# A longer plain stretch around the second norm, its four turns spread one to a round, and outputs split sooner

## The chip, the cores and the metric

The kernel runs on one core of one Trainium2 chip. The metric is the device time of one execution in microseconds (us); lower is better. A core has five engines that run their own instruction streams and meet at semaphores: PE (TensorE, matmuls; its weight loads are told apart as PEld), DVE (VectorE), ACT (ScalarE), POOL (GpSimd) and SP (SyncE, which here only issues DMAs). Sixteen DMA engines serve the queues of SP and POOL.

## What is computed

A transformer block with adaptive layer norms: attention with 32 heads of 16 features over 2048 tokens, then a gated feed-forward part (FFN).

```python
def _A_ref(x, wqkv, wo):              # B, S, D = 1, 2048, 512; H = 32, Dh = 16
    qkv = ... x @ wqkv ...            # q, k, v of every head
    scores = einsum("bhqd,bhkd->bhqk", q, k) * Dh ** -0.5
    o = einsum("bhqk,bhkd->bhqd", softmax(scores), v)
    return o.transpose(...).reshape(B, S, D) @ wo

def _B_ref(x, w_gate, w_up, w_down):  # F = 1792
    return (silu(x @ w_gate) * (x @ w_up)) @ w_down

sa, ca, ga, sb, cb, gb = (silu(c) @ w_mod) in six parts
h = layernorm(x) * (1 + ca) + sa
x = x + ga * _A_ref(h, A_wqkv, A_wo)
h = layernorm(x) * (1 + cb) + sb
x = x + gb * _B_ref(h, B_w_gate, B_w_up, B_w_down)
```

## The kernel before

**Units, steps, pairs.** The queries are cut into four chunks of 512 rows, the heads into eight groups of four. One group of one chunk is a unit; there are 32 units, each with 16 key tiles of 128 keys, so 512 steps in all. A step is four pairs (`pair_of`), one for each head of the group. A pair is two matmuls on PE: a *score* (L612, operands `qop,kop`), whose exponential ACT takes from a PSUM bank into an SBUF tile `pt` or `pu` (L614), and a *maximum* (L563, operands `kop,qop`), a 128x512 product whose row maximum DVE takes (L565). The maxima run 20 steps ahead of the scores, since a unit's row maxima enter its scores as extra rows of `qop`. The counter `done` counts pairs, so `done // 4` is the step.

**Value products.** `pv_step` (L627) multiplies the exponentials with v. It works in halves, one for each 256 queries: four rows of the program, one a head, which the trace shows as eight matmuls. A step owes two halves. All of a unit's 32 halves collect in one bank, bank 70 in the order below. After the last one ACT copies that bank to an SBUF tile `o` (L631), and the next unit's first value product must wait for that copy. `close_unit` then sends the unit's output on: the sums `dn` by DMA on SP (L638), their reciprocal on DVE (L642), through DRAM and back as `rb` (L643, L648), the product with `o` on POOL (L653) and the store in DRAM `o_dr` (L654). After the eighth unit of a chunk the whole chunk's output is read back (`load_o`, L767), 128 rows of 512 for each of four k, and split on POOL into a high part (L772) and a low part (L773), tiles `act`.

**Plain and filled steps.** Steps come in two kinds, and the order on every engine is the order in which this code is written. `plain(steps, tails)` has nothing but attention. It goes in windows of three pairs (`WIN`); after window w it calls `tails[w]` if there is one and then gives out `HALVES[(w - 2) % 4]` halves of value products, HALVES being (2, 1, 1, 2). So four windows are a round: two windows with double halves follow two with single ones. A `pvs` call in a plain step stops at a unit's end and gives the rest out later, so that three pairs stand between a unit's last value product and the next unit's first. `filled(places, work)` lays matmuls of the output projection or the FFN (L829) between the pairs of some steps, at `places`, and gives out all value products of these steps at their end, in one burst, without stopping at a unit's end.

**A chunk's second half.** For each of the first three chunks the main loop runs plain steps until step `STARTS[ci]`; then two `filled_tile` calls of four steps each for the output projection (`out_pair`), after each of which DVE adds the result to the residual `x2` (L860); then a plain stretch of `NORM` steps, in which the second norm is made: sums on ACT, `norm_scale` on DVE and POOL (L785 to L798), four `normalize` on POOL (L807), and four *turns*: PE transposes one k of the normalized rows into a bank that it takes from the maxima's four (L812), ACT scales it (L814), POOL splits it (L815, L816). Then the FFN's 84 filled steps. For the third chunk 12 more plain steps (`REST`) follow the stretch, in a call of their own. Each `plain` call starts its windows at w = 0 and gives one half more in its last window. In the last two windows of a call, and in filled steps, a unit's maxima are brought into `qop` by two DVE instructions and eight DMAs (`max_turned`, L588 to L602), otherwise by three small matmuls, a copy and two DMAs (`max_rows`, L570 to L581).

Of the kernel before, what the change touches and what calls it, by code (L numbers as in the profile page):

```python
# [28 lines left out]
NK = D // P  # L29
NC = 4  # L30
CW = S // NC
NG = H // 4
# [14 lines left out]
FBANKS = (3, 6)  # L47
KEEP = 7
REST = 12
NORM = 18  # L50
STARTS = (147, 275, 403)
TWO = (0, 3, 2, 2, 2, 2, 1, 0)
DOWN = (0, 3, 3, 0, 3, 3, 0, 0)
FOUR = (0, 3, 2, 1, 2, 1, 3, 0, 3, 1, 2, 1, 2, 1, 2, 0)
# [59 lines left out]
def block_kernel(ctx, tc, x, wqkv, wo, w_gate, w_up, w_down, c, w_mod, out):  # L114
    nc = tc.nc
# [422 lines left out]
    last = NC - 1  # L538
# [6 lines left out]
    def load_k(u):  # L545
        load_parts(kop[u % 3], kd, u % NG, 0, S, nc.gpsimd if u > 2 else nc.sync)

    def load_q(u):
        ci, g = divmod(u, NG)
        qop[u] = pb.tile([P, 2, CW], F32R, name="qop", tag="qop", bufs=3)  # L550
        first, second = [(nc.gpsimd, nc.sync)[k] for k in ((0, 0), (1, 1), (1, 0))[min(u, 1) + (u > 2)]]
        load_parts(qop[u], qd, g, ci * CW, (ci + 1) * CW, second, first)
# [81 lines left out]
    def out_a(u, eng):  # L634
        pv.pop(u)
        o = o_.pop(u)
        dn = pf.tile([P, 16], F32, name="dn", tag="dn", bufs=1)
        eng.dma_start(dn, o[16:P:32, :].rearrange("h (b e) -> h b e", e=16))  # L638
        return o, dn

    def out_b(u, eng, o, dn):
        nc.vector.reciprocal(dn, dn)  # L642
        eng.dma_start(d_dr[u].rearrange("h (b e) -> (h b) e", e=16), dn)  # L643
        return o,

    def out_r(u, eng, o):
        rb = pf.tile([P, CW], F32, name="rb", tag="rb", bufs=1)
        eng.dma_start(rb, d_dr[u][:, None, :].to_broadcast([4, 32, CW]))  # L648
        return o, rb

    def out_c(u, eng, mul, o, rb):
        ci, g = divmod(u, NG)
        mul.tensor_mul(rb, o, rb)  # L653
        eng.dma_start(o_dr[ci, g], rb)  # L654

    def at(i, f):
        due.setdefault(i, []).append(f)
# [282 lines left out]
    chunks = {}  # L940
    side = []
    def begin(ci):
        x2 = pf.tile([P, 4, D], F32, name="x2", tag="x2", bufs=1)
        act = [pf.tile([P, NK, CW], F32R, name=f"act{a}", tag=f"act{a}", bufs=1) for a in range(2)]
        hT = [pf.tile([P, NK, CW], F32R, name=f"act{a}", tag=f"act{a}", bufs=1) for a in range(2)]
        chunks[ci] = ch = Chunk(ci, x2, act, hT)
        ch.load_x2(nc.sync if ci else nc.gpsimd)

    def scaled(ch):
        ch.load_gu(0)  # L950
        ch.load_gu(1)
        ch.norm_scale(nc.gpsimd)
        ch.nt = [tile_mid().bitcast(F32) for _ in range(2)]
        for t in range(4):
            ch.normalize(t)
# [17 lines left out]
    def close_unit(u, i):  # L973

        if u == NU - 1:
            res[u] = out_a(u, nc.scalar)
            return
        res[u] = out_a(u, nc.sync)
        if u + 3 < NU:
            load_k(u + 3)  # L980
            load_q(u + 3)
        i0 = i if u % NG == NG - 1 else i + 3
        at(i0 + 3, lambda: res.__setitem__(u, out_b(u, nc.sync, *res[u])))
        at(i0 + 4, lambda: res.__setitem__(u, out_r(u, nc.sync, *res[u])))
        at(i0 + 5, lambda: out_c(u, nc.gpsimd, nc.gpsimd, *res.pop(u)))
        if u % NG == NG - 1:
            if u // NG:
                at(i + 4, lambda: begin(u // NG))
                at(i + 5, lambda: chunks[u // NG].load_wo())
            at(i + 7, lambda: chunks[u // NG].load_o(nc.gpsimd))  # L990
            at(i + 9, lambda: chunks[u // NG].split_o())

    at(3, lambda: begin(0))
    at(UG - 2, lambda: chunks[0].load_wo())
# [31 lines left out]
    def pair_of():  # L1026
        nonlocal done
        i = done // 4 - 1
        most = 4 * n - 4 * (LEAD - 1)
        h = (ORDER if done < most else (0, 1, 2, 3))[done % 4]  # L1030
        work = [lambda: score(i + 1, h)]
        if done < most:
            work.insert(1 - h % 2, lambda: max_one(done + 4 * (LEAD - 1)))
        for f in work:
            f()
        done += 1
        if side:
            side.pop(0)()
# [39 lines left out]
    def pvs(most, by_halves):  # L1078

        nonlocal owed  # L1080
        if by_halves:
            most, owed = most + owed, 0
        while most and halves and 4 * halves[0][0] + 8 <= done:
            i, half = halves.pop(0)
            pv_step(i, half)
            most -= 1
            if i % 16 == 15 and half:
                close_unit(i // 16, done // 4 - 1)
                if by_halves:
                    break  # L1090
        if by_halves and most and halves and 4 * halves[0][0] + 8 <= done:
            owed = most

    def turns_behind():
        for b in list(behind):
            b[0] -= 1
            if not b[0]:
                b[1]()
                behind.remove(b)

    def end_steps():
        nonlocal ended
        while ended < done // 4:
            after(ended - 1)
            ended += 1

    def plain(steps, tails=()):

        nonlocal four, bank, beside
        beside = False  # L1110
        assert steps % WIN == 0 and done % 4 == 0
        four, bank = Turn(0, 3, 1, 2), Turn(4, 5, 6)
        for w in range(4 * steps // WIN):
            beside = w > 4 * steps // WIN - 3
            for _ in range(WIN):
                pair_of()
            if w < len(tails) and tails[w]:
                tails[w](four())
            pvs((HALVES[(w - 2) % 4] if done > 8 else 0) + (w == 4 * steps // WIN - 1), True)
            turns_behind()  # L1120
            end_steps()
# [17 lines left out]
    def filled_tile(job, ch, arg):  # L1139
        one = done // 4 % 16 != 15 and done + 16 <= 4 * n - 4 * (LEAD - 1)  # L1140
        work = job(ch, arg, outs, True, one)
        for places in (FOUR,) if one else (TWO, TWO):
            filled(places, work)
# [14 lines left out]
    for ci in range(last):  # L1158
        plain(STARTS[ci] - done // 4)
        ch = chunks[ci]  # L1160
        for t0 in (0, 2):
            filled_tile(out_pair, ch, t0)
        behind.append([6, lambda: scaled(ch)])
        tails = [None] * 10
        for k in range(NK):
            tails += [lambda tp, k=k: ch.turned(tp, k), None, None]
        plain(NORM, tails)
        if ci == last - 1:
            plain(REST)
        for _ in range(len(ch.jobs) - (KEEP if ci == last - 1 else 0)):  # L1170
            job, args = ch.jobs.pop(0)
            if ci == last - 1 and args == (7,):
                plain(18 - REST)
            if job is gate_up:
                filled_tile(job, ch, *args)
            else:
                filled(DOWN, job(ch, *args, outs, True))
# [25 lines left out]
    ch, chp = chunks[last], chunks[last - 1]  # L1203
# [54 lines left out]
```

## Time and profile before

| | us |
|---|---|
| three timed runs, median (lowest to highest) | 1818.45 (1815.83 to 1818.61) |
| the profiled execution, its own time | 1815.69 |
| its span (first to last instruction) | 1813.9 |

Shares of the span that an engine is busy: PE 99%, weight loads 65%, DVE 83%, ACT 68%, POOL 25%. The granted TensorE clock was 0.999. A busy PE is not a PE at its peak, because matmuls are pipelined and a matmul that waits for its bank counts as begun. So stages are read apart, by what ended the idle time of DVE and of the weight loads in each. Steps 0 to 146 are plain apart from weight preparation that other engines do beside them. The first chunk's output projection begins at 525.8 us, its norm stretch at 552.5 us, its FFN at 599.0 us; for the second chunk at 925.1, 952.1 and 998.7 us, for the third at 1324.6, 1351.4 and (after the 12 further plain steps) 1427.0 us.

### The profile page before, as it was taken

The numbers are of one execution on the slowest core, as the hardware profiler recorded it, in microseconds if no ns is written. First come the engines' busy times: TensorE is split into PE (matmuls) and PEld (weight loads), VectorE is DVE, ScalarE is ACT, GpSimd is POOL, SyncE is SP. The second block draws the span as 40 slices with busy tenths as digits, with TensorE's granted clock in tenths as the row PEclk, the third lists the DMA queues.
The fourth block names the chain that finished last, engine by engine and source line by source line (L and its number), as shares of the span: only waits on it lengthen the run. The fifth ranks groups of instructions, "written<-read, shape, count | busy, mean of one in ns | idle before, by whom it ended". The sixth has DMA issues, their size and how long they took to land.

```text
span 1813.9 us, 41319 instructions
## 1 busy us (share of the span) xinstructions
PE 1803.1 (99%) x17036; PEld 1173.2 (65%) x17036; DVE 1506.5 (83%) x2558; ACT 1232.2 (68%) x2356; POOL 459.1 (25%) x538
## 2 busy tenths in 40 slices
PE   9999999999999999999999999999999999999999
PEld 7876444444455677777564777777564677667887
DVE  5568999999999888888999888888989988922544
ACT  4223888888889767667788766776888867773211
POOL 3612544556223111111133111111123011031200
PEclk9999999999999999999999999999999999999999
DMA  9874876667844554464455555444624555233742
GB/s 310 288 232 142 202 199 175 174 171 199 213 80 104 126 127 120 112 149 98 111 124 122 127 121 128 110 123 102 168 61 104 104 148 123 106 122 117 291 165 101
DMA packets 80705, 267.65 MB, mean 148 GB/s; under 512 B 19884, under 2 KB 24428, under 8 KB 59836
## 3 DMA queue, kind: packets, MB, share of 16 engines
q1 hardware_dynamic: 61540, 179.71, 34.1%
q0 software_dynamic: 18288, 84.49, 19.4%
q8 instruction: 134, 2.20, 0.5%
q10 hardware_dynamic: 688, 0.80, 0.1%
q14 instruction: 55, 0.45, 0.1%
HBM read 201.85 MB, written 62.13 MB: 146 GB/s over the span
## 4 chain that ended last, share of the span: by engine, by line
PE 89%; DVE 9%; ACT 1%; DMA 0%; issue 0%; SPq 0%; DVEq 0%
PE bank L627 24%; PE bank L829 20%; PE bank L612 15%; PE bank L563 13%; DVE mx L565 9%; PE bank L848 8%; PE bank L223 5%; PE bank L466 2%; PE bank L891 1%; PE bank L812 1%; DMA wm_ab<-in_w_mod 0%; PE bank L175 0%; DVE v_flat L924 0%; PE bank L577 0%; SPq L271 0%
## 5 line engine op out<-in xcount | busy, mean ns | idle before, releaser
L565 DVE TENSOR_REDUCE mx<-bank 128x1 f32<-128x512 f32 x2048 | 1259.5, 682 | 113.9 <-PE bank L563 79.7
L563 PE MATMUL bank<-kop,qop 48*128 48x512 f32 x2048 | 733.7, 425 | 0.7
L612 PE MATMUL bank<-qop,kop 50*128 50x512 f32 x2048 | 730.8, 427 | 1.9 <-ACT pt__17687 L614 0.4
L612 PEld LDWEIGHTS bank<-qop,kop 50*128 50x128 f32 x2048 | 345.6, 184 | 196.5 <-issue 34.9
L563 PEld LDWEIGHTS bank<-kop,qop 48*128 48x128 f32 x2048 | 351.1, 184 | 111.6 <-DVE mx L565 68.9
L829 PE MATMUL bank<-act,wgu 64*128 64x512 f32 x1872 | 306.2, 392 | 0.0
L829 PEld LDWEIGHTS bank<-act,wgu 64*128 64x128 f32 x1872 | 190.5, 187 | 17.8
L653 POOL TENSOR_TENSOR rb<-o,rb 128x512 f32<-128x512 f32 x31 | 39.8, 1285 | 436.0 <-DMA rb<-d_dr 349.3
L912 POOL CAST mid<-m 128x512 fp32r<-128x512 f32 x40 | 24.2, 606 | 434.1 <-DVE m L910 434.1
L829 PE MATMUL bank<-wd,mid 64*128 64x512 f32 x912 | 131.4, 391 | 0.0
L829 PEld LDWEIGHTS bank<-wd,mid 64*128 64x128 f32 x912 | 91.5, 186 | 11.7
L908 DVE SCALAR_TENSOR_TENSOR q<-th,bank 128x512 f32<-128x512 f32 x56 | 37.9, 676 | 54.7 <-ACT th L904 54.7
L904 ACT ACTIVATE th<-bank 128x512 f32<-128x512 f32 x56 | 33.5, 598 | 58.4 <-PE bank L848 58.4
L223 PE MATMUL bank<-hT,wqs 128*128 128x512 f32 x300 | 72.4, 395 | 0.4 <-DVE wqs L363 0.4
L924 DVE TENSOR_TENSOR x<-bank,x 128x512 f32<-128x512 f32 x84 | 53.9, 685 | 16.2 <-PE bank L829 16.1
L223 PEld LDWEIGHTS bank<-hT,wqs 128*128 128x128 f32 x300 | 55.4, 188 | 13.8 <-issue 1.0
L910 DVE TENSOR_TENSOR m<-bank,q 128x512 f32<-128x512 f32 x56 | 38.7, 692 | 21.4 <-PE bank L848 19.4
L913 POOL TENSOR_TENSOR mid<-m,mid 128x512 fp32r<-128x512 f32 x40 | 51.3, 1282 | 3.4
L848 PE MATMUL bank<-wd,mid 128*128 128x512 f32 x216 | 51.5, 393 | 0.0
L829 PE MATMUL bank<-wgu,act 64*128 64x512 f32 x288 | 47.9, 393 | 0.0
L848 PEld LDWEIGHTS bank<-wd,mid 128*128 128x128 f32 x216 | 40.3, 188 | 9.1 <-POOL mid L913 0.3
L848 PE MATMUL bank<-kop,kop 128*128 128x512 f32 x192 | 45.4, 393 | 0.0
(6304 smaller groups left out, 5219.7 us busy)
## 6 DMA issues: line engine op xcount, KB each, us to landing
wgu<-gu_dr SPq DMA_DIRECT2D x48, 1024.0 KB
wd<-wd_dr SPq DMA_DIRECT2D x28, 1024.0 KB
kop<-kd SPq DMA_DIRECT2D x33, 768.0 KB
kop<-kd POOLq DMA_DIRECT2D x29, 768.0 KB, 9.3
gu_dr<-wgu POOLq DMA_DIRECT2D x14, 1024.0 KB, 13.5
kd<-prt SPq DMA_DIRECT2D x16, 512.0 KB
qd<-prt SPq DMA_DIRECT2D x16, 512.0 KB
kop<-gu_dr SPq DMA_DIRECT2D x8, 1024.0 KB
```

What stands on the lines that cost most here:

```text
L223: nc.tensor.matmul(pt, lhs(a, k), rhs(b, k), start=(n == 0), stop=(n == 3 * nk - 1))
L563: nc.tensor.matmul(pm, qop[u][rows, s, qt * P:(qt + 1) * P], kop[u % 3][rows, s, kc * CW:(kc + 1) * CW], start=True, stop=True)
L565: nc.vector.tensor_reduce(mx[u][:, b, s, qt, kc:kc + 1], pm, op=ALU.max, axis=AX.X)
L612: nc.tensor.matmul(sp, kop[u % 3][rows, h // 2, kt * P:(kt + 1) * P], qop[u][rows, h // 2, :], start=True, stop=True)
L627: nc.tensor.matmul(pv[u][32 * h:32 * h + 32, cols], v_flat[:, e0:e0 + 32], p_[h][:, cols], start=(kt == 0 and half == 0), stop=(kt == 15), ...
L653: mul.tensor_mul(rb, o, rb)
L829: mm = nc.tensor.matmul(outs[e], lhs(e, a, k)[rows], rhs(b, k)[rows], start=(ph == 0 and j == 0), stop=(j == z and (ph == 1 or trade)), sk ...
L848: nc.tensor.matmul(outs[e], lhs(e, a, k), rhs(b, k), start=(j == 0), stop=(j == z))
L908: nc.vector.scalar_tensor_tensor(q, th, 1.0, outs[0], op0=ALU.add, op1=ALU.mult)
L910: nc.vector.tensor_mul(m32, outs[1], q)
L913: (nc.gpsimd if slow else nc.vector).tensor_sub(mid[:, 1, :], m32, mid[:, 0, :].bitcast(F32))
L924: nc.vector.tensor_add(ch.x2[:, t, :], outs[e], ch.x2[:, t, :])
```

## The change

The three `STARTS` are 3 steps earlier and `NORM` is 3 steps longer, so the FFN begins at the same step as before: what was 147 plain, 8 filled, 18 plain becomes 144, 8, 21. The turns go from windows 10, 13, 16, 19 to 11, 15, 19, 23, which is the first single-half window of each of four rounds. For the third chunk the 21 and the 12 steps become one call of 33. The chunk's object is made earlier (`begin` at i + 1), three quarters of the chunk's output are read back and split at i + 1 and i + 2, and only the last quarter, which holds the last two units, waits for i + 7 and i + 9; the load of `x2` stays at i + 4.

```diff
-NORM = 18
-STARTS = (147, 275, 403)
+NORM = 21
+STARTS = (144, 272, 400)
...
         chunks[ci] = ch = Chunk(ci, x2, act, hT)
-        ch.load_x2(nc.sync if ci else nc.gpsimd)
+        if not ci:
+            ch.load_x2(nc.gpsimd)
...
             if u // NG:
-                at(i + 4, lambda: begin(u // NG))
+                at(i + 1, lambda: begin(u // NG))
+                at(i + 4, lambda: chunks[u // NG].load_x2(nc.sync))
                 at(i + 5, lambda: chunks[u // NG].load_wo())
-            at(i + 7, lambda: chunks[u // NG].load_o(nc.gpsimd))
-            at(i + 9, lambda: chunks[u // NG].split_o())
+            at(i + 1, lambda: chunks[u // NG].load_o(nc.gpsimd, range(NK - 1)))
+            at(i + 2, lambda: chunks[u // NG].split_o(range(NK - 1)))
+            at(i + 7, lambda: chunks[u // NG].load_o(nc.gpsimd, (NK - 1,)))
+            at(i + 9, lambda: chunks[u // NG].split_o((NK - 1,)))
...
-        tails = [None] * 10
+        tails = [None] * 11
         for k in range(NK):
-            tails += [lambda tp, k=k: ch.turned(tp, k), None, None]
-        plain(NORM, tails)
-        if ci == last - 1:
-            plain(REST)
+            tails += [lambda tp, k=k: ch.turned(tp, k), None, None, None]
+        plain(NORM + (REST if ci == last - 1 else 0), tails)
```

Three places show how the instructions stand now. The first is PE at the end of unit 8, whose last key tile falls at step 143 to 145. Before, this is in the plain steps ahead of the output projection:

```order
L627 MATMUL bank_70<-pu__6045,v_flat 32x256
L563 MATMUL bank_64<-kop_971,qop 128x512 [waits DVE_49]
L612 MATMUL bank_67<-qop,kop_88 128x512 [waits Activation_49]
L563 MATMUL bank_65<-kop_971,qop 128x512 [waits DVE_49]
L612 MATMUL bank_68<-qop,kop_88 128x512 [waits Activation_49]
L612 MATMUL bank_69<-qop,kop_88 128x512 [waits Activation_49]
L563 MATMUL bank_63<-kop_971,qop 128x512 [waits DVE_49]
L627 MATMUL bank_70<-pt__6052,v_flat 32x256 [waits Activation_49]
L627 MATMUL bank_70<-pt__6064,v_flat 32x256
```

Now it is in the burst behind the first four filled steps (the same unit's last half, then the next unit's first):

```order
L627 MATMUL bank_70<-pt__6020,v_flat 32x256
L627 MATMUL bank_70<-pt__6040,v_flat 32x256
L627 MATMUL bank_70<-pt__6033,v_flat 32x256
L627 MATMUL bank_70<-pu__6045,v_flat 32x256
L627 MATMUL bank_70<-pt__6056,v_flat 32x256 [waits Activation_49]
L627 MATMUL bank_70<-pt__6074,v_flat 32x256
L627 MATMUL bank_70<-pt__6061,v_flat 32x256
L627 MATMUL bank_70<-pu__6083,v_flat 32x256
```

The wait for ACT's copy stood behind three pairs and now stands directly behind the value product that the copy needs; six halves of the burst and the next filled steps are queued behind it. The same happens at units 16 and 24.

The second place is PE at the first turn of the first chunk. Before, the turn is followed by a double half (these four rows and the same four again):

```order
L563 MATMUL bank_63<-kop_1658,qop 128x512 [waits DVE_49]
L812 MATMUL bank_66<-ident,mid 128x128 [waits DVE_49,Pool_49]
L812 MATMUL bank_66<-ident,mid 128x128 [waits Pool_49] x3
L627 MATMUL bank_70<-pt__6702,v_flat 32x256
L627 MATMUL bank_70<-pt__6714,v_flat 32x256
L627 MATMUL bank_70<-pt__6707,v_flat 32x256
L627 MATMUL bank_70<-pu__6731,v_flat 32x256
```

Now one half follows, and then the next pairs:

```order
L612 MATMUL bank_67<-qop,kop_971 128x512 [waits Activation_49]
L812 MATMUL bank_63<-ident,mid 128x128 [waits DVE_49,Pool_49]
L812 MATMUL bank_63<-ident,mid 128x128 [waits Pool_49] x3
L627 MATMUL bank_70<-pt__6642,v_flat 32x256
L627 MATMUL bank_70<-pt__6662,v_flat 32x256
L627 MATMUL bank_70<-pt__6647,v_flat 32x256
L627 MATMUL bank_70<-pu__6667,v_flat 32x256
L612 MATMUL bank_68<-qop,kop_971 128x512 [waits Activation_49]
L563 MATMUL bank_66<-kop_1658,qop 128x512 [waits DVE_49]
```

Of the four turns before, two stood ahead of double halves and two ahead of single ones; now all four stand ahead of single ones.

The third place is POOL ahead of the first output projection. Before, the product for the chunk's last unit comes first and then the whole chunk is read and split:

```order
L653 TENSOR_TENSOR rb<-o,rb 128x512 [waits DMAHW4_49,DMASW5_49,Activation_49]
L654 DMA o_dr<-rb 128x512 [waits DMASW0_49,Pool_49]
L767 DMA act_1757<-o_dr 128x1x512
L767 DMA act_1757<-o_dr 128x1x512 [waits DMASW2_49]
L767 DMA act_1757<-o_dr 128x1x512 [waits DMASW3_49]
L767 DMA act_1757<-o_dr 128x1x512 [waits DMASW4_49,DMASW0_49]
L772 CAST act_1756<-act_1757 128x512 [waits DMASW1_49]
L773 TENSOR_TENSOR act_1757<-act_1757,act_1756 128x512 [waits Pool_49]
```

Now three loads stand right behind the loads of `kop` and `qop` for the unit three further on, three splits follow them, and only one quarter comes after the product (from the third split on):

```order
L772 CAST act_1756<-act_1757 128x512 [waits DMASW2_49]
L773 TENSOR_TENSOR act_1757<-act_1757,act_1756 128x512 [waits Pool_49]
L653 TENSOR_TENSOR rb<-o,rb 128x512 [waits DMAHW4_49,DMASW5_49,Activation_49]
L654 DMA o_dr<-rb 128x512 [waits DMASW3_49,Pool_49]
L767 DMA act_1757<-o_dr 128x1x512 [waits DMASW4_49,DMASW3_49]
L772 CAST act_1756<-act_1757 128x512 [waits DMASW4_49]
```

Three of the four reads of `o_dr` have moved ahead of the product on POOL's queue, and with them their splits.

## The prediction

> **What bounds the kernel now.** I read the page first: PE has work all the time, and the chain that ended last is PE's, but 9% of it is DVE's maxima. The third row is the group that PE's loads wait for.
>
> ```profile
> PE 1803.1 (99%) x17036; PEld 1173.2 (65%) x17036; DVE 1506.5 (83%) x2558; ACT 1232.2 (68%) x2356; POOL 459.1 (25%) x538
> PE 89%; DVE 9%; ACT 1%; DMA 0%; issue 0%; SPq 0%; DVEq 0%
> L565 DVE TENSOR_REDUCE mx<-bank 128x1 f32<-128x512 f32 x2048 | 1259.5, 682 | 113.9 <-PE bank L563 79.7
> ```
>
> An average over stages hides which engine is late, so I cut the time by stage: plain steps ahead of the first output projection, that projection, and the norm stretch behind it (columns: length, then busy time of PE, weight loads, DVE, ACT, POOL).
>
> ```profile
> 440.00:516.00 76.00, 76.00 (x773) 36.79 (x776) 76.00 (x131) 66.61 (x133) 33.34 (x35) 1.00 0.70 178
> 525.84:552.47 26.63, 26.63 (x294) 19.32 (x290) 22.83 (x39) 22.24 (x45) 1.49 (x2) 1.00 0.35 57
> 552.47:599.00 46.53, 45.98 (x459) 22.20 (x455) 44.60 (x78) 41.74 (x85) 16.59 (x30) 1.00 0.53 126
> ```
>
> In plain steps DVE never rests: 76.00 of 76.00. In the projection it has 3.8 us to spare, and PE sets the pace. In the norm stretch, plain steps as well, DVE loses 1.9 us. The groups by line say what a maximum costs and who ended those waits; the first row is of 440 to 516 us, the second of the norm stretch.
>
> ```profile
> L565 DVE TENSOR_REDUCE mx<-bank 128x1 f32<-128x512 f32 x127 | 76.2, 679 | 0.0
> L565 DVE TENSOR_REDUCE mx<-bank 128x1 f32<-128x512 f32 x72 | 44.3, 683 | 3.4 <-PE bank L563 3.0 <-PE bank L612 0.2
> ```
>
> A maximum takes 76.2 / 127 = 0.60 us and a plain step four of them, 2.4 us. So in plain steps a microsecond counts when DVE is given work or is left without a product; in filled steps, when PE is. DVE's timeline of the turns shows its idle times in brackets, and that of the weight loads where the four turns (L812) stand.
>
> ```profile
> 574.25 5.48 DVE L565 TENSOR_REDUCE mx<-bank 128x1 f32<-128x512 f32 x9 [0.47 <-PE bank L563]
> 580.11 7.53 DVE L565 TENSOR_REDUCE mx<-bank 128x1 f32<-128x512 f32 x12 [0.39 <-PE bank L563]
> 587.56 0.24 DVE L642 RECIPROCAL dn<-dn 128x16 f32<-128x16 f32 x1
> 587.74 3.83 DVE L565 TENSOR_REDUCE mx<-bank 128x1 f32<-128x512 f32 x6
> 591.75 1.89 DVE L565 TENSOR_REDUCE mx<-bank 128x1 f32<-128x512 f32 x3 [0.18 <-PE bank L612]
> ...
> 572.10 0.42 PEld L812 LDWEIGHTS bank<-ident,mid 128*128 128x128 f32 x4 [0.48 <-POOL mid L807]
> 577.98 0.42 PEld L812 LDWEIGHTS bank<-ident,mid 128*128 128x128 f32 x4 [0.41 <-DVE mx L565]
> 584.06 0.42 PEld L812 LDWEIGHTS bank<-ident,mid 128*128 128x128 f32 x4 [0.24 <-DVE mx L565]
> 590.02 0.42 PEld L812 LDWEIGHTS bank<-ident,mid 128*128 128x128 f32 x4 [0.37 <-DVE mx L565]
> ```
>
> The two turns ahead of double halves (572.10, 577.98) leave DVE idle for 0.47 and 0.39 us; the two ahead of single ones for nothing and for 0.18. The first also waited 0.48 us for POOL's normalized rows.
>
> **The change, term by term.** *The turns.* Before, 0.47 + 0.39 + 0.18 = 1.04 us a chunk. After, all four stand as the last two did, which cost 0.18 together, 0.09 each: 0.36 us. The first is a window later and no longer early for POOL. That gives back 0.68 us a chunk, 2.0 for three. Ends: every turn costs 0.18 (gain 0.32 a chunk, 1.0 in all), or none costs anything (3.1).
>
> *The unit's end that moves into a burst.* Units 8, 16 and 24 end some two steps behind the new start of the projection, so their last value product, before in plain steps, lies inside a burst. What PE does at such an end today, in plain steps (first row), and how long the copy takes when it follows a burst with nothing between (the other rows):
>
> ```profile
> 921.97 0.11 PEld L627 LDWEIGHTS bank<-pt__11309,v_flat 128*32 128x32 f32 x1 [0.37 <-ACT o L631]
> ...
> 611.97 0.38 PE L627 MATMUL bank<-pt__7173,v_flat 128*32 128x256 f32 x1
> 612.18 0.38 PE L627 MATMUL bank<-pt__7173,v_flat 128*32 128x256 f32 x1
> 612.65 0.59 ACT L631 COPY o<-bank 128x512 f32<-128x512 f32 x1 [2.70 <-PE bank L627]
> ```
>
> Value passes follow each other by 0.21 us (611.97, 612.18), so the next would begin at 612.39; the copy ends at 612.65 + 0.59 = 613.24. In a burst PE would stand 0.85 us, and the projection is the stage where PE sets the pace: +0.85 a chunk, +2.6 in all. Ends: nothing, if it costs as little as the 0.37 us wait in plain steps, which DVE's work covers; and 0.85 + 0.59 = 1.4 a chunk, 4.3 in all, if the copy finds ACT in another instruction of its size. I take the middle row, the only one with copy and burst side by side.
>
> *The unit's output chain, three steps later.* The reciprocal of units 8, 16 and 24 falls into plain steps instead of filled ones. From 587.56 to the next maximum at 587.74 it costs DVE 0.18 us: +0.5 for three, between 0 and 0.5.
>
> *The third chunk's joined call.* Where the 18 steps ended and 12 began, DVE's timeline has this:
>
> ```profile
> 1398.51 0.69 DVE L565 TENSOR_REDUCE mx<-bank 128x1 f32<-128x512 f32 x1 [0.37 <-PE bank L563]
> 1399.12 0.17 DVE L593 SCALAR_TENSOR_TENSOR parts<-m,parts 128x16 fp32r<-128x16 f32 x1
> 1399.32 0.21 DVE L595 STREAM_TRANSPOSE turned<-parts 128x32 f32<-128x32 f32 x1
> 1399.46 3.04 DVE L565 TENSOR_REDUCE mx<-bank 128x1 f32<-128x512 f32 x5
> ```
>
> The extra half of the last window goes (0.37 us), and away from a call's end the maxima are brought over by matmuls, so two DVE instructions go (1399.12 to 1399.46, 0.34). PE's three small matmuls come instead, in steps where it has some time; I take -0.6, between 0 and -0.7.
>
> *What costs nothing.* The 3 steps leave one plain stretch and join another: 3 x 2.4 us less and more. POOL's three early splits, 5.8 us a chunk, lie beside plain steps in which it is busy 33 of 76 us. For the fourth quarter the question is whether it comes in time; the second chunk has the least room (POOL's timeline, then that of the loads and of PE where the projection begins, then POOL's of the first chunk):
>
> ```profile
> 915.83 0.59 POOL L767 DMA_DIRECT2D act<-o_dr  x1 [5.52 <-DMA o_dr<-rb]
> 916.41 0.63 POOL L772 CAST act<-act 128x512 fp32r<-128x512 f32 x1
> DMA to landing us min/median/max: 4.1/4.1/4.1
> 925.14 0.18 PEld L612 LDWEIGHTS bank<-qop,kop 50*128 50x128 f32 x1 [0.67 <-ACT pu__11395 L614]
> 929.42 0.87 PE L829 MATMUL bank<-wgu,act 64*128 64x512 f32 x6
> ...
> 518.78 1.28 POOL L773 TENSOR_TENSOR act<-act,act 128x512 fp32r<-128x512 f32 x1
> ```
>
> The last read is issued at 915.83 and lands 4.1 us later, at 919.9. Now its split follows at once: the high part is there at 919.9 + 0.63 = 920.5. PE wants this quarter in the group of six at 929.42, which is 4.3 us behind the projection's first step at 925.14. With a start three steps (7.2 us) earlier that is 922.2. So 1.7 us of room and no wait. In the first chunk (last row) the last split ended at 520.1; without the three ahead of it that is 514.3, and the new start is at 525.8 - 7.2 = 518.6.
>
> *Sum.* -2.0 + 2.6 + 0.5 - 0.6 = +0.5 us. Against the profiled execution's own 1815.69 (span 1813.9 and 1.8 around it) that is 1816.2. The three timed runs, 1818.45, 1815.83 and 1818.61, are 1817.63 on average, so a median can come from either end; I predict 1817.63 + 0.5 = 1818.1. The terms' ends add to -3.3 (0 - 3.1 + 0.5 - 0.7) and +3.8 (4.3 - 1.0 + 0.5 + 0).
>
> **The rivals.** *Slower: a small transfer behind the early reads.* The three early reads, 768 KB, now enter POOL's queue with the loads of `kop` and `qop`, in the very microseconds in which `dn` of the chunk's last unit is fetched. Rows of that window, the second chunk's:
>
> ```profile
> DMA packets 818, 2.52 MB, mean 158 GB/s; under 512 B 353, under 2 KB 353, under 8 KB 625
> kop<-kd POOLq DMA_DIRECT2D x1, 768.0 KB, 9.6
> 882.00 0.58 POOL L487 DMA_DIRECT2D qop<-qd  x1 [0.15 <-issue]
> L638 SPq DMA_DIRECT2D dn<-o x1: 589/589/589, 882.1 to 882.1; - x1
> L642 DVEq EVENT_SEMAPHORE  x1: 21/21/21, 891.2 to 891.2; - x1
> L642 DVE RECIPROCAL dn<-dn x1: 244/244/244, 892.9 to 892.9; 128x16 f32<-128x16 f32 x1
> ```
>
> DVE's sequencer found `dn` landed at 891.2, the reciprocal began at 892.9: 1.7 us of room at least. At 158 GB/s 768 KB take 4.9 us. If `dn` waits for all of it, DVE stands 3.2 us in a plain step, 9.6 for three chunks: 1828. It decides from 1.7 us of delay on. For it: `kop` itself needed 9.6 us. Against: POOL would issue the reads from 882.6 on, SP issued `dn` at 882.1, half a microsecond ahead. The Trainium skill (DMA: Bandwidth & Descriptors, Queues, rings and completion order) says that an engine takes turns between queues, a packet from each; by it `dn` would wait for one packet of POOL's queue at most, and the sum stays 1818.1. The trace has it land 9.1 us after its issue or sooner, which does not settle it. I give one chance in eight to a delay that counts, mostly a partial one (1821 to 1824).
>
> *Faster: no burst stall.* If PE's wait in the burst is made up, because the filled steps behind it have waits of their own that shrink, the 2.6 go, and with turns that cost nothing another 1.1: 1818.1 - 3.7 = 1814.4. For it: DVE has 3.8 us to spare in the projection. Against: PE is busy 26.63 of 26.63 us there, so there is little wait to shrink.
>
> *The turns keep their cost.* A turn holds PE's loads for 0.42 us wherever it stands, and if a round with a turn is longer for PE than for DVE, each costs 0.18 us: 1818.1 + 1.0 = 1819.1. This lies inside the forecast.
>
> **Chances.** 0.2% of this kernel is 3.6 us, about what a measurement can tell from no change. No change, 0.74: the sum lies within +-3.6 unless both big terms lie at one end. Faster, 0.13: the second rival. Slower, 0.13: the first, or a burst stall at its upper end with small gains. The range goes from 1815.69 - 2.0 = 1813.7, low terms on a run at the low end, to 1818.61 + 3.3 = 1821.9, high terms on a run at the high end or part of the first rival.
>
> **What would show it.** Right, if in each of the three projections the burst has a weight load of L627 behind ACT's copy with some 0.85 us of idle time; if DVE's idle times at the turns fall from 1.04 to about 0.4 us a chunk; if DVE's time from the out tiles to the FFN holds one more reciprocal; and if at the third chunk's step 429 the 0.37 us and L593 and L595 are gone. Wrong, if DVE waits for `dn` (a gap ahead of L642), or PE for `act` in the projection (a gap ahead of L829 ended by POOL), or if the stall in the burst is absent.

## The result, and the profile after

The changed kernel takes 1828.14 us (median of six runs, 1825.43 to 1835.05), the kernel before 1816.66 us (median of six, 1815.4 to 1818.61). The ratio is 1.007, with a 95% interval of 1.0049 to 1.0091: it is slower, by 11.5 us. The profiled execution took 1828.14 us, its span is 1826.4.

The page of after has the same busy times as before, and in the shares of the chain a share of DMA that was not there:

```profile
PE 1808.2 (99%) x17042; PEld 1171.3 (64%) x17042; DVE 1507.5 (83%) x2556; ACT 1232.3 (67%) x2357; POOL 459.4 (25%) x538
PE 85%; DVE 8%; DMA 4%; issue 1%; ACT 1%; POOL 0%; SPq 0%; POOLq 0%; ACTq 0%; DVEq 0%
L565 DVE TENSOR_REDUCE mx<-bank 128x1 f32<-128x512 f32 x2048 | 1259.6, 680 | 120.0 <-PE bank L563 80.9
```

Cut by stage as before (plain steps ahead of the first projection, the projection, the norm stretch), the plain steps are the ones that changed: DVE was busy 76.00 of 76.00 us there, now 70.23 of 77.00, and the granted clock (the value ahead of the last two) fell from 1.00 to 0.93.

```profile
448.00:525.00 77.00, 73.20 (x710) 34.74 (x710) 70.23 (x121) 60.96 (x121) 29.59 (x32) 0.93 0.62 160
526.04:553.59 27.55, 26.80 (x292) 19.00 (x288) 22.78 (x38) 22.71 (x46) 0.60 (x2) 1.00 0.48 74
553.59:607.00 53.41, 53.08 (x530) 24.93 (x526) 51.80 (x91) 47.74 (x97) 18.03 (x31) 1.00 0.46 114
```

DVE's timeline around the reciprocal L642 of units 7, 15 and 23 names the wait: `dn`. It is 4.43 us in the first chunk, 1.99 in the second, none in the third. Behind the first, DVE waits three times more, for PE:

```profile
489.82 4.26 DVE L565 TENSOR_REDUCE mx<-bank 128x1 f32<-128x512 f32 x7
498.52 0.25 DVE L642 RECIPROCAL dn<-dn 128x16 f32<-128x16 f32 x1 [4.43 <-DMA dn<-o]
498.69 3.61 DVE L565 TENSOR_REDUCE mx<-bank 128x1 f32<-128x512 f32 x6
502.56 1.89 DVE L565 TENSOR_REDUCE mx<-bank 128x1 f32<-128x512 f32 x3 [0.27 <-PE bank L563]
505.12 1.89 DVE L565 TENSOR_REDUCE mx<-bank 128x1 f32<-128x512 f32 x3 [0.67 <-PE bank L612]
508.36 3.82 DVE L565 TENSOR_REDUCE mx<-bank 128x1 f32<-128x512 f32 x6 [1.36 <-PE bank L563]
...
903.04 0.25 DVE L642 RECIPROCAL dn<-dn 128x16 f32<-128x16 f32 x1 [1.99 <-DMA dn<-o]
...
1303.47 0.24 DVE L642 RECIPROCAL dn<-dn 128x16 f32<-128x16 f32 x1
```

Busy times in short stretches tell why PE was late there: while DVE waited, PE stood still, and then its clock was at half speed for ten microseconds. Behind the second wait it stayed whole.

```profile
494.00:496.00 2.00, 1.57 (x20) 0.60 (x18) 0.09 (x1) 1.71 (x4) 0.00 (x0) 1.00 1.05 181
496.00:498.00 2.00, 0.00 (x0) 0.00 (x0) 0.00 (x0) 0.20 (x1) 0.61 (x1) 0.93 1.11 150
498.00:508.00 10.00, 8.63 (x50) 3.50 (x52) 7.55 (x13) 4.34 (x8) 4.97 (x6) 0.50 0.38 76
508.00:510.00 2.00, 2.00 (x24) 1.00 (x26) 1.64 (x3) 1.57 (x3) 1.19 (x1) 1.00 0.01 3
...
905.00:915.00 10.00, 9.94 (x98) 4.64 (x98) 10.00 (x18) 8.43 (x17) 5.57 (x6) 1.00 0.58 129
```

The list of who waited for whom on PE (total, times, longest) has PE's share of the two waits for `dn` (first row), and two more waits that the kernel before has nowhere: the three copies in the bursts, and a wait for `qop` in the third chunk.

```profile
PE bank L563 <- DVE mx L565: 5.2, 2, 3.8
PE bank L627 <- ACT o L631: 2.2, 3, 0.8
PE bank L612 <- DMA qop<-mr: 1.2, 1, 1.2
```

The start of each step's first score, in the two traces, shows how far after lies behind before, and where that grew:

| from step to step | what lies there | behind, us | grew by |
|---|---|---|---|
| 134 to 143 | reciprocal of unit 7 | 0.06 to 7.29 | +7.2 |
| 143 to 155 | first projection, with its burst | to 8.25 | +1.0 |
| 155 to 173 | norm stretch, four turns | to 8.05 | -0.2 |
| 256 to 270 | reciprocal of unit 15 | 8.08 to 10.13 | +2.0 |
| 270 to 283 | second projection | to 11.11 | +1.0 |
| 283 to 301 | norm stretch | to 10.91 | -0.2 |
| 398 to 411 | third projection | 10.99 to 12.29 | +1.3 |
| 411 to 426 | norm stretch, wait for `qop` | to 13.46 | +1.2 |
| 426 to 433 | the joined call | to 12.77 | -0.7 |
| 433 to the end | | to 12.45 | -0.3 |

### The profile page after: what moved, and what is told of

The parts are those of the page before. It is cut to its first block, busy times and chain, and to the rows that moved or that the text cites. A ratio compares the mean times of both kernels' runs of the same rounds, so it can differ in the third digit from the quotient of the medians.

```text
span 1826.4 us, 41318 instructions
## 1 busy us (share of the span) xinstructions
PE 1808.2 (99%) x17042; PEld 1171.3 (64%) x17042; DVE 1507.5 (83%) x2556; ACT 1232.3 (67%) x2357; POOL 459.4 (25%) x538
## 4 chain that ended last, share of the span: by engine, by line
PE 85%; DVE 8%; DMA 4%; issue 1%; ACT 1%; POOL 0%; SPq 0%; POOLq 0%; ACTq 0%; DVEq 0%
PE bank L627 23%; PE bank L829 19%; PE bank L612 15%; PE bank L563 12%; PE bank L848 8%; DVE mx L565 8%; PE bank L223 5%; PE bank L466 2%; DMA dn<-o 1%; DMA act<-o_dr 1%; PE bank L891 1%; DMA wm_ab<-in_w_mod 1%; PE bank L812 0%; DMA o_dr<-rb 0%; DMA rb<-d_dr 0%
```

## The experiments

**The early reads alone, on the kernel before.**

```diff
-                at(i + 4, lambda: begin(u // NG))
+                at(i + 1, lambda: begin(u // NG))
+                at(i + 4, lambda: chunks[u // NG].load_x2(nc.sync))
...
-            at(i + 7, lambda: chunks[u // NG].load_o(nc.gpsimd))
-            at(i + 9, lambda: chunks[u // NG].split_o())
+            at(i + 1, lambda: chunks[u // NG].load_o(nc.gpsimd, range(NK - 1)))
+            at(i + 2, lambda: chunks[u // NG].split_o(range(NK - 1)))
+            at(i + 7, lambda: chunks[u // NG].load_o(nc.gpsimd, (NK - 1,)))
+            at(i + 9, lambda: chunks[u // NG].split_o((NK - 1,)))
```

> The kernel before (1816.7 us) with the early reads alone: three quarters of a chunk's output are read at i + 1 and split at i + 2, the chunk's object is made at i + 1; STARTS, NORM and the turns stay as before. Theory (dn is late behind the early reads, and the wait of 4.4 us in the first chunk also halves PE's granted clock for some 10 us): the loss at these places, 7.4 us in the first chunk and 2.0 us in the second, appears whole, 1816.7 + 9.4 = about 1826, with an idle time of 4 to 5 us ahead of DVE's reciprocal L642 in the first chunk, about 2 us in the second, and a granted clock of 0.50 for some 10 us behind the first. If the wait comes without the clock: 1816.7 + 6.4 = 1823. Rival (the reads alone do nothing, it takes the earlier start of the projection too): within 1 us of 1816.7, no idle time ahead of L642.

1829.33 us (ratio 1.0065, 1.0047 to 1.0083), 12.9 more than before. The two waits are there, a little longer, and this time the clock fell behind the second too (last row), which the 1826 did not hold:

```profile
499.52 0.25 DVE L642 RECIPROCAL dn<-dn 128x16 f32<-128x16 f32 x1 [5.12 <-DMA dn<-o]
903.83 0.25 DVE L642 RECIPROCAL dn<-dn 128x16 f32<-128x16 f32 x1 [2.76 <-DMA dn<-o]
906.00:914.00 8.00, 8.00 (x50) 3.46 (x50) 5.52 (x10) 3.99 (x9) 5.53 (x6) 0.50 0.48 122
```

So the reads alone bring both waits and a loss of this size; the longer plain stretch is not needed for it.

**The early reads on SP's queue.**

```diff
-            at(i + 1, lambda: chunks[u // NG].load_o(nc.gpsimd, range(NK - 1)))
+            at(i + 1, lambda: chunks[u // NG].load_o(nc.sync, range(NK - 1)))
```

> The changed kernel (1828.1 us) with the three early reads issued by SP instead of POOL, so that they stand in SP's queue behind dn and behind SP's halves of kop and qop. Theory (dn waits because POOL's queue is served ahead of it): dn lands as in the kernel before, the idle time ahead of L642 is gone in all chunks, the granted clock is 0.999, and the time falls by 9.4 us to about 1818.7; what is left over the kernel before is the stall in three bursts (0.95 each), a wait of 1.6 us for qop in the third chunk, and the gains of the turns. Rival (the 768 KB make dn late from whatever queue they come): dn still lands 3 us or more late in the first chunk and the time stays above 1823. Second rival: rb, now behind the reads on SP's queue, comes late and PE waits for the fourth quarter at the projection: 1 to 3 us a chunk, 1821 to 1828.

1821.22 us (1.0021, 1.0011 to 1.0031). No idle time ahead of L642 in the three chunks, clock 1.0, though 2.5 us more than the theory's 1818.7. The profiled run, 1820.05, lies 4.4 above that of before. PE's waits are the bursts and, as the second rival had it in a small size, the fourth quarter in the second and third chunk (0.41 and 0.62 us):

```profile
PE bank L627 <- ACT o L631: 2.2, 3, 0.7
PE bank L829 <- POOL act L773: 1.0, 2, 0.6
```

**One quarter on POOL's queue, two on SP's.**

```diff
-            at(i + 1, lambda: chunks[u // NG].load_o(nc.gpsimd, range(NK - 1)))
+            at(i + 1, lambda: (chunks[u // NG].load_o(nc.gpsimd, (0,)),
+                               chunks[u // NG].load_o(nc.sync, range(1, NK - 1))))
```

> The changed kernel (1828.1 us) with one early read of 256 KB left on POOL's queue and the other two on SP's. In the changed kernel DVE's sequencer found dn at 498.5 us in the first chunk, with 768 KB ahead, and with all reads on SP's queue it had no wait. Theory (dn waits for what was given to POOL's queue by then, so its delay goes with the bytes): a third of the delay of some 6 us, 2 us, of which about 1.7 are room: an idle time ahead of L642 of 0 to 0.5 us in the first chunk, no drop of the clock, about the time of the kernel with all reads on SP's queue, 1821 to 1822. Rival (any read on POOL's queue makes dn wait for the whole of its backlog once more, or the delay comes from the bytes on both queues): an idle time of 2 us or more, 1824 to 1828.

1826.65 us (1.0055, 1.004 to 1.0071): the rival's numbers. DVE waited 2.31 us in the first chunk, in the others not at all, and the clock fell behind that wait:

```profile
497.42 0.25 DVE L642 RECIPROCAL dn<-dn 128x16 f32<-128x16 f32 x1 [2.31 <-DMA dn<-o]
499.00:504.00 5.00, 5.00 (x28) 2.09 (x30) 4.17 (x8) 2.66 (x6) 2.56 (x4) 0.50 0.41 134
```

My size was wrong: from issue to the moment DVE's sequencer found it, `dn` took at most 7.4 us before, 11.5 here and 13.6 in the changed kernel, so a third of the bytes brought some 4.1 of the 6.2 us.

**dn on POOL's queue, ahead of the reads.**

```diff
-        res[u] = out_a(u, nc.sync)
+        res[u] = out_a(u, nc.gpsimd if u % NG == NG - 1 else nc.sync)
```

> The changed kernel (1828.1 us) with dn of a chunk's last unit issued by POOL, in the same queue as the loads of kop and qop and the early reads and ahead of them; nothing else moves. Theory (order on the queue that is served first decides): dn lands some 2 to 4 us behind its issue, the idle time ahead of L642 is gone in all chunks, the clock is 0.999, about 1818.7 us; kop, qop and the reads start at most 5 us later than in the changed kernel. Rival (so many bytes under way make a transfer of small pieces late in any queue): dn lands 8 us or more behind its issue, 1823 or above.

1823.1 us (1.0033, 1.0021 to 1.0046). In the second and third chunk the wait is gone, in the first it is 3.23 us: neither text. With `dn` away, SP issued its halves of `kop` and `qop` 7.2 and 5.5 us ahead of `dn`, and now these went first:

```profile
478.05 0.34 SPq L487 DMA_DIRECT2D kop<-kd  x1
479.74 0.32 SPq L487 DMA_DIRECT2D qop<-qd  x1
485.21 0.72 POOL L638 DMA_DIRECT2D dn<-o  x1 [7.56 <-ACT o L631]
497.36 0.25 DVE L642 RECIPROCAL dn<-dn 128x16 f32<-128x16 f32 x1 [3.23 <-DMA dn<-o]
```

In the second and third chunk SP's halves stood about as far ahead, but between the issue of `dn` and its landing only 4 and 11 of SP's records of 2 KB or more were served; in the first chunk, where two loads of `wgu` stood on SP's queue as well, it was 169. So neither queue is always preferred: what had been given ahead and was not yet served went first, whichever queue it came by. One place does not fit this, the second chunk of the changed kernel; it is taken up below.

**The reads on POOL's queue, but behind ACT's copy**, which `dn` waits for as well.

```diff
...
+                if self.gate and k == 0:
+                    tc.add_manual_dep(d.ins, self.gate, SYNC, reason="reads behind the last unit")
...
-            nc.scalar.copy(o_[u], pv[u])
+            copies[u] = nc.scalar.copy(o_[u], pv[u]).ins.name
...
+            at(i + 1, lambda: setattr(chunks[u // NG], "gate", copies[u]))
```

> The changed kernel (1828.1 us) with the first of the early reads, and so all three, waiting on POOL for ACT's copy L631 of the chunk's last unit, which is what dn waits for on SP. In the first chunk the reads are then issued from 484.9 us on, with dn and no longer 3.8 us ahead of it; in the other chunks they were issued behind that copy already, so nothing changes there. Theory A (the engines of the DMA serve what came to them first, from either queue, and a transfer issued by POOL comes to them some 1.5 us later than one issued by SP): in the first chunk dn goes ahead of the reads, the idle time ahead of L642 falls from 4.4 to at most the 2.0 us that the second chunk shows, and 4 to 7 us are gained, 1821 to 1824. Theory B (POOL's queue is served as long as it has anything, and the reads join kop and qop, which run until 490 us): dn still waits for the reads, 4 us and a clock of 0.50, and the time stays near 1828.

1819.75 us (1.0019, 1.0009 to 1.0028), better than theory A asked: the wait is gone from all chunks. In the first chunk the reads were issued 0.26 us behind `dn`, and that was enough. (L640, L644 and L769 of this kernel are L638, L642 and L767 of the changed one. No run shows the 1.5 us of theory A.)

```profile
485.24 1.84 POOL L769 DMA_DIRECT2D act<-o_dr  x3 [4.03 <-ACT o L631]
...
484.98 0.61 SPq L640 DMA_DIRECT2D dn<-o  x1
494.08 0.26 DVE L644 RECIPROCAL dn<-dn 128x16 f32<-128x16 f32 x1
```

The profiled execution took 1823.34 us, 3.6 above the median: in the third chunk PE waited 1.34 us for `qop`, and its clock was halved for 10.24 us behind that.

The trace's records of single DMA packets put these runs side by side. `dn` is 128 pieces of 64 bytes; `kop` and `qop` of POOL are 144 records of 4 or 8 KB, each read of a quarter is 64 of 4 KB (records of a few bytes are left out). For the first chunk:

| kernel | records given to POOL's queue ahead of `dn` | records of that queue served before the middle piece of `dn` | us from issue of `dn` to that piece |
|---|---|---|---|
| before | 144 | 139 | 5.7 |
| reads behind the copy | 144 | 132 | 4.6 |
| one quarter | 208 | 199 | 8.1 |
| changed | 336 | 317 | 11.2 |

**The reads behind the reciprocal**, on POOL's queue.

```diff
-        nc.vector.reciprocal(dn, dn)
+        r = nc.vector.reciprocal(dn, dn)
+        if u % NG == NG - 1 and u < NU - 1:
+            ch = chunks[u // NG]
+            ch.gate = r.ins.name
+            ch.load_o(nc.gpsimd, range(NK - 1))
+            ch.gate = None
...
-            at(i + 1, lambda: chunks[u // NG].load_o(nc.gpsimd, range(NK - 1)))
-            at(i + 2, lambda: chunks[u // NG].split_o(range(NK - 1)))
+            at(i + 4, lambda: chunks[u // NG].split_o(range(NK - 1)))
```

(With the dependency in `load_o` of the run behind ACT's copy.)

> The changed kernel (1828.1 us) with the three early reads still on POOL's queue, but waiting for the reciprocal L642 of the chunk's last unit, so that dn has landed when they are issued; their splits follow at i + 4. Theory (the whole loss at L642 comes from the reads that went ahead of dn): no idle time ahead of L642 in any chunk, the clock at 1.00 there, and about the time of the kernel with the reads on SP's queue, 1818.5 to 1821.5. Rival (the reads now meet d_dr and rb of the same unit, and the fourth quarter is late for the projection): PE waits 1 to 3 us a chunk for the split of the fourth quarter, 1822 to 1828.

1819.51 us (1.0019, 1.0007 to 1.003), no idle time ahead of L642. The rival's wait for the fourth quarter did not come; PE waited for `qop`, 1.2 us in the second chunk and 0.6 in the third. The three runs without the wait (reads on SP's queue, behind the copy, behind the reciprocal) leave 2.9 to 4.8 us of the change's 11.5.

**DVE held up without any DMA, on the kernel before.**

```diff
-        nc.vector.reciprocal(dn, dn)
+        for _ in range({7: 9, 15: 15, 23: 21}.get(u, 1)):
+            nc.vector.reciprocal(dn, dn)
```

> The kernel before (1816.4 us) with DVE held up at the same three places without any DMA: the reciprocal L642 of units 7, 15 and 23 is done 9, 15 and 21 times in a row (an odd number, so the value stays), 8, 14 and 20 more than before, by 0.20 to 0.24 us each 1.6 to 1.9, 2.8 to 3.4 and 4.0 to 4.8 us. In the runs so far PE stood about 0.6 us less than DVE was held, so here about 1.1, 2.5 and 3.8 us. Theory (a pause of PE of about 2 us or more halves its granted clock for some 7 to 10 us, which costs 3 us more, whatever made the pause; one of 1.4 us does not): no drop of the clock at the first place, a drop to 0.50 at the second and the third, time lost about 1.8 + (3.1 + 3) + (4.4 + 3) = 15 us, 1831 to 1832. Rival (the clock fell in the changed kernel for another reason, such as the transfers under way; a pause costs only itself): no drop, 9.2 us lost, 1825 to 1826.

1834.58 us (two runs; 1.0096, 1.0078 to 1.0115). A repeat took 0.29 us (last row: (6.00 - 0.24) / 20), so the holds were 2.3, 4.0 and 5.8 us, 12.1 in all, and the rival's sum would be 1828.8. The other 5.8 us go with the clock, which fell in all three places, behind the short pause for 3.41 us, behind the others for 10.24. So no added transfer is needed for it. (L643 is L642 of the kernel before.)

```profile
497.09 0.49 PE L563 MATMUL bank<-kop,qop 48*128 48x512 f32 x1 [1.57 <-DVE mx L565]
498.00:501.00 3.00, 3.00 (x20) 1.24 (x22) 3.00 (x6) 1.90 (x5) 0.00 (x0) 0.52 0.06 13
901.00:911.00 10.00, 10.00 (x58) 3.99 (x62) 7.51 (x13) 5.33 (x11) 1.38 (x2) 0.50 0.65 203
1307.00:1317.00 10.00, 7.31 (x40) 3.03 (x44) 8.83 (x20) 4.29 (x8) 0.01 (x1) 0.50 0.40 124
1303.10 6.00 DVE L643 RECIPROCAL dn<-dn 128x16 f32<-128x16 f32 x21
```

**Shorter holds:** the same edit with 5, 7 and 11 reciprocals.

> The kernel before with DVE held up by 5, 7 and 11 reciprocals for units 7, 15 and 23 in place of one, 4, 6 and 10 more than before, by the 0.25 us that each took in the run with 9, 15 and 21: 1.0, 1.5 and 2.5 us. PE's pause was up to 0.4 us shorter than the hold there, so here some 0.6, 1.2 and 2.2 us. Theory (the clock drops when PE pauses for more than a length between 1.36 us, which left it at 1.00, and 1.57 us, which brought 0.50): no drop at the first two places, one at the third, time lost 1.0 + 1.5 + 2.5 and some 3 for the clock, about 8 us, 1824 to 1825. Rival (no fixed length decides; the clock falls by chance of where a pause lies): a drop behind one of the first two as well, 1826 to 1829, or none behind the third, 1821 to 1822.

1827.76 us (three runs; 1.0056, 1.0039 to 1.0072). The rival's first case came: behind the second hold PE paused only 0.99 us, and the clock fell all the same, for 3.41 us. In this trace it fell once more, at 1409.33 us and for 3.41 us, where none of PE's waits just before was longer than 0.30 us.

```profile
896.20 0.49 PE L563 MATMUL bank<-kop,qop 48*128 48x512 f32 x1 [0.99 <-DVE mx L565]
898.00:901.00 3.00, 3.00 (x20) 1.25 (x18) 2.94 (x5) 1.57 (x3) 0.00 (x0) 0.54 0.05 7
1299.52 0.49 PE L563 MATMUL bank<-kop,qop 48*128 48x512 f32 x1 [2.14 <-DVE mx L565]
1300.00:1307.00 7.00, 6.90 (x44) 2.87 (x46) 6.07 (x11) 4.34 (x8) 0.00 (x0) 0.51 0.47 129
```

**The 21 steps with STARTS as before**, so that units end inside the FFN's bursts.

```diff
-NORM = 18
+NORM = 21
...
-                plain(18 - REST)
+                plain(15 - REST)
```

(With the changed kernel's `tails` and its joined call.)

> The kernel before (1816.7 us) with the 21 steps and the four turns one to a round, but STARTS as before, so that the FFN begins three steps later, and the last plain stretch is three steps shorter; reads as before. Now no unit ends in the burst of the projection, but in the FFN 15 units (11 to 16, 19 to 24, 28 to 30, by the first value product) end inside a burst where before they ended at the end of one. Theory (a unit's end inside a burst costs 0.95 us, the copy of its bank, at a place where PE sets the pace): 15 x 0.95 = 14.3 us more, less 1.2 us for the turns and 0.6 us for the joined call: about 1829, with an idle time of PE ended by L631 in each of these bursts. Rival (PE makes such a wait up in the filled steps behind it, since there are other waits to shrink): 1814 to 1818.

1826.55 us (1.0056, 1.0041 to 1.0071), 10.1 more than before, between the two texts' times. The mechanism is the theory's, with 0.7 us in place of 0.95: PE waited in each of the 15 bursts, and made nothing of it up (10.6 less the 1.8 us of the gains would be 8.8):

```profile
PE bank L627 <- ACT o L631: 10.6, 15, 0.7
```

**The turns and the joined call alone, on the kernel before.**

```diff
-        tails = [None] * 10
-        for k in range(NK):
-            tails += [lambda tp, k=k: ch.turned(tp, k), None, None]
-        plain(NORM, tails)
-        if ci == last - 1:
-            plain(REST)
+        tails = [None] * 20
+        for k, at_ in enumerate((11, 15, 16, 19)):
+            tails[at_] = lambda tp, k=k: ch.turned(tp, k)
+        plain(NORM + (REST if ci == last - 1 else 0), tails)
```

> The kernel before (1816.4 us) with two parts of the change alone: the four turns stand at windows 11, 15, 16 and 19, all of them windows with single halves, and the third chunk's 18 and 12 steps are one call; STARTS, NORM and the reads stay. Theory (turns behind single halves cost less): DVE's idle time at the turns falls from 1.04 us a chunk to 0.5 to 0.7, worth 1.0 to 1.6 us in all, and the joined call 0.6 us: 1814 to 1815. Rival (a turn holds PE for the same time wherever it stands, and two turns in neighbouring windows wait for POOL's splits): 1816 to 1818.

1813.19 us (0.9979, 0.997 to 0.9987): faster than both kernels, by 3.5 us against before. DVE's idle times at the turns of the first chunk are 0.18, 0.13 and 0.17 us, together 0.48 in place of 1.04; the first of them:

```profile
582.99 3.91 DVE L565 TENSOR_REDUCE mx<-bank 128x1 f32<-128x512 f32 x6 [0.18 <-PE bank L612]
```

Step by step against before, the three norm stretches are shorter by 0.55, 0.60 and 0.60 us and the joined call by 0.70: 2.4 us, the lower end of the interval (2.4 to 5.4). What makes the rest is not shown.

**Three repairs of the changed kernel:** the reads on SP's queue, the halves that end a unit given out behind the first filled step, and the first `wgu` loads four windows later.

```diff
-        ch.load_gu(0)
-        ch.load_gu(1)
...
-            at(i + 1, lambda: chunks[u // NG].load_o(nc.gpsimd, range(NK - 1)))
+            at(i + 1, lambda: chunks[u // NG].load_o(nc.sync, range(NK - 1)))
...
+            if first and r == 3:
+                pvs(4, True)
         hook()
-        pvs(len(places) // 2 + 2, False)
+        pvs(len(places) // 2 + (-2 if first else 2), False)
...
+        behind.append([10, lambda: (ch.load_gu(0), ch.load_gu(1))])
```

> The changed kernel with three repairs: the early reads on SP's queue, as in the run of that name (1821.2 us); the four halves that end units 8, 16 and 24 are given out behind the first filled step of the projection, so that three filled steps lie between them and the burst, which has six halves left; and the loads of the first two gate and up weights wait four windows longer, so that qop's maxima of the third chunk stand ahead of them on SP's queue. Theory (the stall in the burst, 0.95 us a chunk, and the wait for qop, 1.4 to 1.6 us in the third chunk, are what is left besides the late fourth quarter of the third chunk, 1.5 us): 1821.2 - 2.9 - 1.4 = about 1817, no idle time of PE ended by L631 in the three bursts, none ended by L581. Rival (the halves given out early cost the projection as much as the stall, since PE sets the pace there and changes between kinds of matmuls once more): 1819 to 1821.

1815.04 us (0.9988, 0.9979 to 0.9997), 1.7 less than before and below the theory's 1817. PE has no wait for L631 and none for `qop` left. The order on SP's queue in the third chunk (first two rows) is again that of the kernel before; in the changed kernel (the rows behind, from its own timeline) two loads of 1 MB and `rb` went ahead of the 8 KB for `qop`:

```profile
1360.69 1.12 SPq L581 DMA_DIRECT2D qop<-mr  x2
1361.91 0.82 SPq L757 DMA_DIRECT2D wgu<-gu_dr  x2
```

```profile
1365.33 1.60 SPq L757 DMA_DIRECT2D wgu<-gu_dr  x2
1367.26 0.56 SPq L648 DMA_DIRECT2D rb<-d_dr  x1
1372.07 1.13 SPq L581 DMA_DIRECT2D qop<-mr  x2
```

All three repairs are in one run, so what each is worth is read from the waits alone.

## Why the prediction was wrong

**The step that failed is the first rival's "Against".** By it the sum put the early reads' effect on `dn` at nothing. It set SP's issue of `dn` (882.1) half a microsecond ahead of POOL's reads (from 882.6), by the second chunk, and let that stand for all three. The trace of before had the first chunk too:

```profile
480.50 0.58 POOL L487 DMA_DIRECT2D qop<-qd  x1
484.84 0.61 SPq L638 DMA_DIRECT2D dn<-o  x1
```

POOL does not wait there for the unit's end; it was 4.3 us ahead of SP. In the changed kernel it put the three reads into that gap (481.12 to 482.96, `dn` at 484.90), and they were served first: a wait of 4.43 us, and with the clock 7.2 of the 12.45 us. Given 0.26 us later than `dn` instead, the reads cost nothing there.

In the second chunk the order was the one that the prediction had, and the wait of 1.99 us came all the same:

```profile
890.18 0.59 SPq L638 DMA_DIRECT2D dn<-o  x1
890.63 1.84 POOL L767 DMA_DIRECT2D act<-o_dr  x3
```

The last five of the 128 pieces of `dn` began as late as 11.0 us after its issue, the others within 9 us; in the kernel before, all began within 8.4 us. In the run with the reads alone 15 pieces were late in this place. But the third chunk, with 0.44 us between `dn` and the reads, had no late piece, nor had the second chunk of the run behind ACT's copy, with 0.67 us. So the reads are what made `dn` late here too, and being given first did not always protect it; why it did in one place and not in the other stays open.

The prediction took the rule of the Trainium skill (DMA: Bandwidth & Descriptors, Queues, rings and completion order) for a wait of one packet, and did not say how much a packet is. The Trainium skill calls a packet there typically 9 to 17 descriptors, at most 64. If a record of the trace is a descriptor, that allows what was measured in the first chunk: after `dn` was issued, 235 records of POOL's queue went ahead of its first piece and 284 ahead of its middle one, 15 to 18 for each of the 16 engines.

**The price of the wait was too small.** I had 3.2 us for a whole delay. The wait was 4.43 us, and the halved clock behind it, which the prediction did not hold at all, brought the loss to 7.2 us. That my 1828 for this rival agrees with the measured time is luck: it is met by 7.2 + 2.0 + 0, not by three times 3.2, and by some 3 us more elsewhere.

**The unit's end in a burst** was right in place and size: 0.75 us of PE's idle time for the 0.85, in all three projections, 0.7 in the fifteen of the FFN. The projections grew by 1.0 to 1.3 us each. The rival that PE makes it up fell.

**The turns** were right in direction, but the sum took too much for them. DVE's idle times in the first chunk fell from 1.04 to 0.68 us, not to 0.36: each of the four turns costs 0.14 to 0.19, the upper end that I gave, and so the third rival is right on this term. (The three below; the first, 0.14 us at 576.89, is too short for the merged timeline to print.) The first turn's wait for POOL is gone, as said. The reciprocal of unit 8 now stands in the norm stretch, at 561.62 us, as said as well; 0.36 us back and its 0.18 us spent are the -0.2 by which the stretch changed.

```profile
584.57 7.43 DVE L565 TENSOR_REDUCE mx<-bank 128x1 f32<-128x512 f32 x12 [0.19 <-PE bank L612]
592.17 3.68 DVE L565 TENSOR_REDUCE mx<-bank 128x1 f32<-128x512 f32 x6 [0.17 <-PE bank L563]
...
599.80 4.31 DVE L565 TENSOR_REDUCE mx<-bank 128x1 f32<-128x512 f32 x7 [0.18 <-PE bank L612]
```

**The joined call** gained about what was said (-0.7 for -0.6), and L593 and L595 are gone there. In the sum of the terms' ends the reciprocal stands with 0.5 at the low end too, where its own low end is 0: -3.8, not -3.3; nothing hung on it.

**What costs nothing** missed two things: the FFN's first weight loads are issued three steps earlier as well, ahead of `qop` on SP's queue, which cost 1.2 us of PE's time in the third chunk; and the second chunk's 1.7 us of room did not hold for the third, where the last split ended at 1333.2 us; the weight loads waited 0.53 us for it, PE itself some 0.1.

## What to carry to other kernels

Before a transfer is moved ahead of a wait, look up for every place where the code runs when each queue really issues: an engine with nothing to wait for runs microseconds ahead (4.3 us here), and what it gives to the DMA engines can go ahead of the small transfer that somebody waits for. Hang the large transfer on the event that releases the small one, as the run behind ACT's copy did, or on its use, as the run behind the reciprocal did; here either took the waits away in all three chunks. And count a pause of PE as longer than it is, for the clock that it may take along.

## What the hardware showed

A pause of PE of one microsecond can halve its granted clock. In the thirteen traces, apart from each kernel's start and end, eleven pauses were followed by a clock of 0.50: they measured 0.99, 1.34, 1.57, 1.67, 2.12, 2.14, 2.61, 3.29, 3.80, 4.48 and 5.01 us. Pauses of 0.94, 0.99, 1.17, 1.21 (twice), 1.36 and 1.47 us were not followed by it, nor were the waits of 0.70 to 0.75 us in the bursts, nor waits for a weight some 11 us after the kernels' start, of up to 1.72 us. So from 2.12 us on the clock fell each time, and between 0.99 and 1.72 us it went either way. Once it fell without a pause of more than 0.30 us. What decides is not shown.

The clock's own record has a grid: every stretch at half speed away from start and end lasted 3.41, 6.83 or 10.24 us, which is one, two or three times 3.41, and the stretches at full speed between two of them are whole multiples of 3.41 us too. The Trainium skill (TensorE: Matmul & The Clock Gate, Part 1: The HAM clock gate) names an idle window of about 3.4 us that runs free of the program. The half speed and the grid agree with it, but pauses well under 3.4 us were enough here.

The scatter of the times goes with the clock: the six runs of the changed kernel have mean clocks from 0.993 to 0.998, and the two slowest, 1834.06 and 1835.05 us, have the lowest (0.995 and 0.993). That their clock fell in more places is likely, but there is no trace of them.
